# A decode attention kernel: GpSimd instead of SyncE coordinates the entry and the exit of its critical section

## Chip, cores and metric

One core of one Trainium2 chip. The metric is device time in microseconds (us), the median of several executions. The "span" of a profile runs from the first to the last recorded instruction and is some 2 us shorter than the time. The threshold is 2%, which is 13 us here.

## The reference

```python
# x: (2, 1, 512); k_cache, v_cache: (2, 32, 8192, 128) bf16; wq: (512, 4096); wo: (4096, 512)
def reference(A_x, A_k_cache, A_v_cache, A_wq, A_wo, B_x, B_w1, B_w2):
    xn = layernorm(A_x)
    q = (xn @ A_wq) split into 32 heads
    p = softmax(q @ k_cache^T * 128 ** -0.5)
    attention = (p @ v_cache, heads joined) @ A_wo
    mlp = relu(xn @ B_w1) @ B_w2
    return A_x + attention + mlp
```

This is one decode step: the caches, 268 MB, are read once, and little is computed with each byte.

## The kernel before

The whole body stands in one critical section: there the author places instructions and semaphores on the engines by hand, and the framework adds only an entry and an exit. One engine coordinates these two; without an argument it is SyncE. The parts that matter (cuts marked):

```python
    ctx.enter_context(tc.tile_critical(no_gpsimd_drain=True))      # line 63
    # ... tiles, semaphores
    def load_k(t):
        nc.sync.dma_start(ks[t % R][:], K_all[...]).then_inc(dK[t % R], 16)
    nc.sync.dma_start(vs[1][:], A_wq...).then_inc(dV[1], 16)       # SyncE's first transfer, line 168
    # ... SyncE: all loads of K and V, then
        sp.wait_ge(sE, 1)
        sp.dma_start(out..., osb[:]).then_inc(dO, 16)              # the output, line 201
    # GpSimd: setup (memsets, identity matrices), then
        g.wait_ge(sV, 100)
        for t in range(NP):                                        # 32 small copies
            if t >= R:
                g.wait_ge(sS, t - R + 1)
            g.tensor_copy(q2[t % R][:], qb[:, 2 * t:2 * t + 2]).then_inc(sQ1, 1)
        g.wait_ge(dO, 16).then_inc(sG, 1)     # waits for the output's landing, line 238
    # ... TensorE, VectorE, ScalarE: the computation, in loops over 32 blocks
```

As built, the coordinator does this: at the entry a NOP on it (an instruction that here only waits for or sends a signal) tells all engines that they may start. At the exit it first signals that it is through its own part; every engine then drains and signals back; the coordinator waits for these signals and goes on. After that comes the launch's own ending, on line 587 in the profile: a barrier that GpSimd collects and releases (its "collecting wait" is the wait for the other engines' signals), a clearing of semaphores on GpSimd (EVENT_SEMAPHORE_RANGE_CLEAR), and a second barrier.

## Time and profile before

| | before |
|---|---|
| time, median of 3 runs | 661.26 us (661.19 to 661.27) |
| span of the profile | 659.3 us |
| read from memory | 280.5 MB, DMA share 1.00 at 431 GB/s from 34 to 626 us |
| SyncE's first transfer issued | 0.970 us (ScalarE's 2 KB input at 0.922) |
| output issued / landed | 656.759 / 657.950 us |
| GpSimd's wait for it over / the barrier's collecting wait | 657.974 / 658.257 us |
| from the collecting wait to the end of the span | 1.079 us |

The lines of the profile that this rests on are in the prediction below. Times with three decimals are starts of single records in the trace.

### The profile page before, as it was taken

Reading aid. Unit: us, or ns where it says so; the run is one execution under the profiler, and the core shown is the slowest. Engines: PE = TensorE matmul, PEld = TensorE weight load, DVE = VectorE, ACT = ScalarE, POOL = GpSimd, SP = SyncE. Lnnn points to the kernel's source line nnn. Section 1 sums busy time; section 2 is a strip of 40 time slices with the busy share of each in tenths; the row PEclk is TensorE's granted clock in tenths of the full one; section 3 lists DMA queues with packets and bytes.
Section 4 is the critical chain, followed back from the end, with each engine's and each line's share of the span. In section 5 each row is a group of like instructions: output and inputs, shape, how many; then the busy total and the mean of one; then the engine's idle time right before and its main releaser. Section 6 shows DMA issues by size and latency. Waiting matters only on the chain.

```text
span 659.3 us, 26888 instructions
## 1 busy us (share of the span) xinstructions
PE 562.9 (85%) x12747; PEld 538.3 (82%) x12747; DVE 253.4 (38%) x437; ACT 255.9 (39%) x403; POOL 9.0 (1%) x46
## 2 busy tenths in 40 slices
PE   2998899988799787889888788979787998788796
PEld 0488898988799787888888788978787988788795
DVE  1054344433344343334434334434333444334341
ACT  1043444444334433344343434434243444334340
POOL 1000000000000000000000000000000000000000
PEclk9798899989989898999889899979899989889998
DMA  8999999999999999999999999999999999999996
GB/s 363 447 417 437 419 437 429 431 439 423 439 423 435 431 429 439 423 439 423 435 435 427 441 419 439 427 431 437 425 441 419 439 427 431 437 425 441 421 426 266
DMA packets 10670, 280.66 MB, mean 426 GB/s; under 512 B 1250, under 2 KB 1252, under 8 KB 1828
## 3 DMA queue, kind: packets, MB, share of 16 engines
q1 hardware_dynamic: 10656, 280.50, 99.1%
q8 instruction: 9, 0.15, 0.1%
q14 instruction: 1, 0.01, 0.0%
q10 hardware_dynamic: 4, 0.00, 0.0%
HBM read 280.50 MB, written 0.00 MB: 425 GB/s over the span
## 4 chain that ended last, share of the span: by engine, by line
DMA 56%; PE 39%; ACT 2%; issue 1%; SPq 0%; DVE 0%; ACTq 0%
DMA ks<-in_A_k_cache_dram 50%; PE tp L300 21%; PE Sc L307 11%; DMA w_sb<-in_A_wo_dram 4%; PE ot L320 4%; DMA vs<-in_A_wq_dram 2%; ACT kT L427 2%; PE ot L252 1%; PE Sc L285 1%; PE ot L266 1%; ACT L427 1%; SPq L199 0%; PE Sc L355 0%; PE Sc L358 0%; SPq L194 0%
## 5 line engine op out<-in xcount | busy, mean ns | idle before, releaser
L300 PE MATMUL tp<-identb,ks 128*128 128x128 bf16 x4096 | 326.0, 229 | 68.2 <-DMA ks<-in_A_k_cache_dram 67.4
L427 DVE COPY kT<-tp 128x1024 bf16<-128x1024 bf16 x320 | 219.8, 691 | 325.1 <-PE tp L300 324.9
L300 PEld LDWEIGHTS tp<-identb,ks 128*128 128x128 bf16 x4096 | 257.2, 103 | 72.1 <-DMA ks<-in_A_k_cache_dram 70.5
L427 ACT COPY kT<-tp 128x1024 bf16<-128x1024 bf16 x192 | 194.3, 1012 | 233.4 <-PE tp L300 233.4
L307 PE MATMUL Sc<-q,kT 128*128 128x64 bf16 x4096 | 216.6, 196 | 4.6 <-ACT kT L427 4.6
L307 PEld LDWEIGHTS Sc<-q,kT 128*128 128x128 bf16 x4096 | 178.8, 100 | 7.9 <-ACT kT L427 7.8
L320 PE MATMUL ot<-prm,vs 128*128 128x64 bf16 x4224 | 156.1, 192 | 4.7 <-issue 4.7
L320 PEld LDWEIGHTS ot<-prm,vs 128*128 128x128 bf16 x4224 | 139.0, 97 | 7.5 <-issue 4.9
L542 ACT COPY nm<-Sc 128x2 f32<-128x2 f32 x32 | 5.1, 160 | 118.4 <-PE Sc L358 118.4
L546 ACT ACTIVATE prm<-Sc,nm 64x128 bf16<-64x128 f32 x64 | 25.6, 401 | 4.3
L483 DVE TENSOR_REDUCE mcol<-Sc 64x1 bf16<-64x128 f32 x64 | 18.6, 291 | 17.6 <-PE Sc L307 17.2
L427 ACT ACT_TABLE_LOAD x16 | 20.5, 1283 | 2.2
L252 PE MATMUL ot<-vs,xz 128*16 128x512 bf16 x32 | 9.3, 462 | 8.8 <-DMA vs<-in_A_wq_dram 8.8
L534 ACT COPY OTf<-ot 128x2 f32 x32 | 5.1, 160 | 27.3 <-PE ot L320 27.3
L488 DVE TENSOR_REDUCE mx<-Sc 1x2 bf16<-1x128 bf16 x32 | 8.9, 279 | 16.9 <-PE Sc L355 16.9
L252 PEld LDWEIGHTS ot<-vs,xz 128*16 128x16 bf16 x32 | 3.3, 103 | 14.4 <-issue 12.0
L237 POOL COPY q<-qb 128x2 bf16<-128x2 bf16 x32 | 5.9, 187 | 590.8 <-PE Sc L307 567.5
L546 ACT ACTIVATION_READ_ACCUMULATOR prm<-Sc,nm x64 | 11.8, 185 | 0.0
L457 DVE TENSOR_SCALAR qs<-ot 16x512 bf16<-16x512 f32 x1 | 0.7, 678 | 17.9 <-PE ot L252 17.9
L355 PE MATMUL Sc<-identb,mcol 128*1 128x128 bf16 x32 | 7.0, 217 | 0.0
L285 PE MATMUL Sc<-w_sb,hT 128*2 128x512 bf16 (+1 forms) x16 | 6.0, 544 | 0.1
L358 PE MATMUL Sc<-mx,onesb 1*128 1x2 bf16 x32 | 5.5, 172 | 0.0
(56 smaller groups left out, 38.6 us busy)
## 6 DMA issues: line engine op xcount, KB each, us to landing
ks<-in_A_k_cache_dram SPq DMA_DIRECT2D x32, 4096.0 KB, 26.7
vs<-in_A_v_cache_dram SPq DMA_DIRECT2D x31, 4096.0 KB, 31.3
vs<-in_A_wq_dram SPq DMA_DIRECT2D x1, 4096.0 KB, 12.3
vs<-in_A_v_cache_dram SPq DMA_DIRECT2D x2, 2048.0 KB, 20.0
w_sb<-in_B_w_dram SPq DMA_DIRECT2D x1, 1792.0 KB, 16.1
w_sb<-in_A_wo_dram SPq DMA_DIRECT2D x1, 1792.0 KB, 26.0
w_sb<-in_B_w_dram SPq DMA_DIRECT2D x1, 1536.0 KB, 19.3
w_sb<-in_A_wo_dram SPq DMA_DIRECT2D x1, 896.0 KB, 27.7
```

Of the source, the lines that this page charges most:

```text
L237: g.tensor_copy(q2[t % R][:], qb[:, 2 * t:2 * t + 2]).then_inc(sQ1, 1)
L252: i = pe.matmul(qp, lhsT=xz[:, kt, Z - g * Bsz:Z - g * Bsz + QG * Bsz], rhs=vs[1][:, (kt * QG + g) * 512:(kt * QG + g + 1) * 512], start=( ...
L266: i = pe.matmul(hp[0:HP if j >= FA else P, j, :], lhsT=w1_b[:, kt, j - FA, :] if j >= FA else w1_a[:, kt, j, :], rhs=xz[:, kt, Z:Z + Bsz], ...
L285: i = pe.matmul(y, lhsT=hT[half, j, :], rhs=w2_sb[half, j, :], start=(j == 0), stop=(j == FJ - 1),)
L300: t = pe.transpose(tp[e % 4][:, i, :], ks[r][:, kk * Dh:(kk + 1) * Dh], identb[:])
L307: t = pe.matmul(Sc[r][:, 2 * kk:2 * kk + 2 * REP], lhsT=kT[e % 4][:, i, :], rhs=rep(q2[r][:]), start=True, stop=True,)
L320: t = pe.matmul(ot[r][:, 0:2 * REP], lhsT=vs[r][:, kk * Dh:(kk + 1) * Dh], rhs=rep(prm[r][:, kk, :]), start=(kk == 0), stop=(kk == KB - 1),)
L355: pe.transpose(tr_of(r), mcol[r][:], identb[:]).then_inc(sT, 1)
L427: fn(kT[e % 4][:], tp[e % 4][:]).then_inc(kR[e], 1)
L483: m = v.tensor_reduce(out=mcol[i][half, :], in_=S_of(i)[half, :, u], axis=AX.X, op=ALU.max)
L488: v.tensor_reduce(out=mx[i][:], in_=tr_of(i).rearrange("o (u m) -> o u m", u=2), axis=AX.X, op=ALU.max, negate=True,).then_inc(sX, 1)
L546: x = a.activation(out=prm[i][half, :, u], in_=S_of(i)[half, :, u], func=ACTF.Exp, bias=nm[i][half, u:u + 1], scale=1.0, accum_out=RS[half ...
```

## The change

GpSimd coordinates instead of SyncE. The likely intent: GpSimd has little to do and in any case waits for the output at the end, while SyncE issues nearly all the transfers.

```diff
-    ctx.enter_context(tc.tile_critical(no_gpsimd_drain=True))
+    ctx.enter_context(tc.tile_critical(sync_engine=mybir.EngineType.Pool, no_gpsimd_drain=True))
```

The built programs differ in this: SyncE loses its entry NOP and gets other waits at the end. GpSimd gets the entry NOP and the exit's signal, waits and NOP. The other engines keep their instructions and wait for another semaphore.

## The prediction

> **What bounds the kernel now.** I read four things in this order: the slices of the whole span on the page, a table of four stretches, the chain of waits at both ends, and the records of the few source lines that the change can touch. First the slices, each digit a fortieth of the span:
>
> ```profile
> POOL 1000000000000000000000000000000000000000
> DMA  8999999999999999999999999999999999999996
> ```
>
> The DMA engines are 90% or more busy in 38 of 40 slices; GpSimd (POOL) does its setup in the first slice and then next to nothing. The table of stretches (start:end, length, busy time and number of instructions of each engine, granted clock, DMA share, GB/s) sharpens that:
>
> ```profile
> 0.00:34.00 34.00, 20.70 (x139) 10.23 (x140) 4.16 (x14) 3.34 (x5) 3.44 (x16) 0.90 0.96 402
> 34.00:322.00 288.00, 253.82 (x5891) 247.31 (x5889) 118.81 (x200) 121.15 (x190) 2.80 (x15) 0.95 1.00 431
> 322.00:626.00 304.00, 260.92 (x6064) 254.68 (x6061) 120.81 (x204) 124.07 (x197) 2.80 (x15) 0.94 1.00 431
> 626.00:660.00 34.00, 27.42 (x661) 26.07 (x661) 9.60 (x20) 7.30 (x12) 0.00 (x0) 0.85 0.81 340
> ```
>
> From 34 to 626 us the DMA share is 1.00 at 431 GB/s. The kernel reads 280.50 MB, and 280.50 MB / 431 GB/s = 650.8 us of the 659.3 us span. TensorE is behind, with 88% busy in the second stretch and 86% in the third. So the stream of K and V blocks sets the time. Anything that moves the start of the first transfer moves the whole stream, and anything after the last transfer is added at the end. Everything between is bound by something that the change does not touch.
>
> The chain of waits at the start (start us, length, what) shows what stands ahead of the first transfer:
>
> ```profile
> 0.73 0.02 SPq L63
> 0.75 0.07 issue
> 0.81 0.03 SPq L587
> 0.85 0.12 issue
> 0.97 12.30 DMA vs<-in_A_wq_dram
> ```
>
> Line 63 is the line that the change edits: the critical section. SyncE's NOP of line 63 at 0.73 us signals the entry, SyncE's own branch (line 587) starts at 0.81 and the first weights' transfer is issued at 0.97. At the other end, the last work and the records of lines 63, 238 and 587 (engine operation xcount: duration min/median/max in ns, first and last start in us):
>
> ```profile
> 656.76 0.32 SPq L201 DMA_DIRECT2D out_dram<-osb  x1
> ```
>
> ```profile
> L238 POOLq EVENT_SEMAPHORE  x1: 17/17/17, 658.0 to 658.0; - x1
> ```
>
> ```profile
> L63 SPq EVENT_SEMAPHORE  x3: 17/28/28, 657.1 to 657.5; - x3
> L63 SPq NOP  x2: 18/18/18, 0.7 to 658.1; - x2
> L63 ACTq DRAIN  x1: 8/8/8, 657.2 to 657.2; - x1
> L63 SPq DRAIN  x1: 127/127/127, 657.2 to 657.2; - x1
> L63 POOLq NOP  x1: 13/13/13, 658.1 to 658.1; - x1
> ```
>
> The output is issued at 656.76 us; GpSimd's wait for its landing (line 238) is over at 658.0. The exit work of the other engines (line 63 drains, at 657.2) is done meanwhile, hidden under the output's flight.
>
> **What the Trainium skill says.** "Advanced Engine Details and Errata", section Clock Domains, gives SyncE's and GpSimd's sequencers the same 1.2 GHz, so a NOP or a semaphore instruction should cost the same on either; the trace agrees (an EVENT_SEMAPHORE is 17 ns on both; a NOP 18 ns on SyncE, 13 on GpSimd). "Perfetto Trace Analysis", section Sequencer-only Instruction, says that the profile shows only the execution of such an instruction, and that the wait and the propagation of its semaphore lie outside: the trace agrees (the NOP ends at 0.747 us, other engines' branches start at 0.770), so hops must be counted from start to start, not by durations. "DMA: Bandwidth & Descriptors", section Anatomy of one DMA, puts most of a transfer's fixed cost into the receipt of the write, some 2 us for its own path; here the output of 2 KB, on a SyncE queue, takes 1.19 us from issue to its last landing (656.759 to 657.950). That is the time that hides the old exit.
>
> **The change part by part.** Compared as built, the programs of TensorE, VectorE and ScalarE keep all their instructions and only wait on another semaphore. SyncE loses the entry's NOP and gains waits at its end; GpSimd gains the entry's NOP and the collecting waits of the exit. No instruction of the main loop changes, no transfer is added or moved to another queue. The times below are starts of single records in the trace.
>
> Entry, before: GpSimd already collects the launch barrier and releases it at 0.621; SyncE wakes at 0.664, runs the NOP at 0.729, the others' branches start at 0.770 (41 ns later), SyncE's own at 0.814 (85 ns later, since it waits for its own signal), its DMA at 0.970 (156 ns after the branch). Entry, after: GpSimd runs the NOP itself, with no wake of SyncE between. On GpSimd, a semaphore instruction, two branches and then a NOP are 95 ns apart at the end of this trace (657.974 to 658.069), and a semaphore instruction to the next instruction 78 to 81 ns. With 90 ns as an estimate, the NOP is at 0.621 + 0.090 = 0.711. SyncE now waits for another engine's signal, 40 ns (GpSimd's NOP at 658.069, SyncE's NOP at 658.109): branch at 0.751, DMA at 0.907. That is 0.970 - 0.907 = 0.06 us earlier. GpSimd instead waits for its own signal: branch near 0.711 + 0.085 = 0.796 in place of 0.772, so its setup is 0.02 us later; it is done by 4.3 us and TensorE's next wait, for the weights, ends at 13.3, so this is off the path.
>
> Exit, before: after the landing, GpSimd's wait 657.974, its NOP 658.069, SyncE's NOP 658.109, SyncE's drains 658.162 and 658.225, GpSimd's collecting wait of the closing barrier 658.257. From NOP to collecting wait 0.19 us. Exit, after: where the NOP stood at 658.069, GpSimd first signals that it has left the section, and only now do the other engines run the drains that were hidden before. Their drains would start 38 to 45 ns later (as after SyncE's signal at 657.144: 657.182 to 657.189) and be seen after another 30 or so, in parallel. GpSimd itself runs in order: signal at 658.069, own NOP 78 ns later (658.147), two waits on two semaphores each. SyncE's such waits stand 74 ns apart (657.419, 657.493); the first 50 ns after the NOP (658.197), the second at 658.273, the last NOP at 658.35, a branch and a drain at 658.40, the collecting wait 79 ns after (as 659.074 to 659.153), about 658.48. Against 658.257 this is 0.22 us later. SyncE's own new waits (two, 74 ns each, and two drains) end near 658.41 by the same steps, so GpSimd sets it. The 0.9 us from there to the end (barrier, clearing of semaphores, barrier) is the same.
>
> Sum: -0.06 + 0.22 = +0.16 us. 661.26 + 0.16 = 661.42, say 661.4 us, a change of 0.02%.
>
> **The rivals.** (a) The saving at the entry counts and the exit costs nothing, because the other engines' drains are as good as free and GpSimd is quicker through its waits than I took from SyncE: -0.06 us, 661.2. For it: GpSimd was already the last to arrive, waiting for the output; against it: the round trip through the other engines is now serial, after the landing. (b) GpSimd is slow as a coordinator, with some 0.2 us for each step instead of 0.08, as its 157 ns drain in the closing barrier hints: six steps at 0.12 more would add 0.7 us, 662.1. Against it: its semaphore instructions stand 78 to 81 ns apart, the same as SyncE's 74. (c) The 0.06 us shift at the start moves the phase between TensorE and the transfers, or the granted clock falls otherwise (mean 0.938), and the stream loses or wins some tenths. Against it: the DMA share is 1.00 for 592 us, so the phase has little to give, and three runs lie within 0.08 us of each other. It could give 0.5 us either way. (d) The old exit held the span by SyncE's 127 ns drain, which would vanish: against it, that drain ended at 657.35, over 0.6 us before GpSimd's wait.
>
> **Range and chances.** The known parts span 661.2 (a) to 662.1 (b); rival (c) adds a few tenths on either side and favours neither. I take 660.7 to 662.2 for 8 in 10. 2% would be 13 us; both ends together, from the start of the span to the first transfer and from the output's issue to the end, are 0.97 + 2.58 = 3.55 us, so a gain of 2% can not come out of them at all, and a loss would need a hang-like delay. Faster 0.01, same 0.98, slower 0.01.
>
> **What would show it.** In the profile after: the first SyncE DMA near 0.91 us instead of 0.97; the NOP of line 63 at the entry on GpSimd near 0.71; the line 63 drains of ScalarE, VectorE and TensorE no longer at 657.2, under the output's flight, but just after GpSimd's line 238 wait; from that wait's start to the end of the span 1.36 us (657.974 to 659.336) grown to about 1.58; DMA share still 1.00 at 431 GB/s in the two middle stretches, and the output's issue 0.06 us earlier. The prediction is wrong if the exit grows by less than 0.1 or over 0.5 us, if SyncE's first DMA is not earlier, or if the output's issue moves by over 0.3 us, which would mean that the stream itself changed.

## The result

The changed kernel takes 661.96 us (median of 5 runs, 661.83 to 662.06), before 661.27 us in the same rounds (5 runs, 661.19 to 661.34). The ratio, the mean time of one kernel's fast runs over that of the other's of the same rounds and so not quite the ratio of these medians, is 1.0009, 95% interval 0.9997 to 1.0022: the same within 2%. The medians differ by 0.69 us where 0.16 was expected.

The table of stretches after the change (columns as in the prediction) shows the same stream:

```profile
34.00:322.00 288.00, 251.75 (x5903) 245.15 (x5900) 119.07 (x201) 121.54 (x190) 2.80 (x15) 0.96 1.00 431
322.00:626.00 304.00, 260.83 (x6067) 254.54 (x6063) 120.90 (x204) 124.07 (x197) 2.80 (x15) 0.94 1.00 431
```

The chain of waits at the start, of the kernel after:

```profile
0.62 0.02 POOLq L576
0.64 0.06 issue
0.70 0.02 POOLq L63
0.73 0.02 issue
0.74 0.03 SPq L587
0.78 0.12 issue
0.90 12.49 DMA vs<-in_A_wq_dram
```

GpSimd's NOP stands at 0.70 us and follows directly on its release of the launch barrier (line 576, at 0.62); SyncE's first transfer is issued at 0.90 in place of 0.97. At the other end, the output and the records of lines 238 and 63 after:

```profile
656.66 0.32 SPq L201 DMA_DIRECT2D out_dram<-osb  x1
```

```profile
L238 POOLq EVENT_SEMAPHORE  x1: 17/17/17, 657.9 to 657.9; - x1
```

```profile
L63 POOLq NOP  x3: 13/13/13, 0.7 to 658.3; - x3
L63 POOLq EVENT_SEMAPHORE  x3: 17/43/43, 658.0 to 658.2; - x3
L63 SPq DRAIN  x1: 7/7/7, 658.0 to 658.0; - x1
L63 ACTq DRAIN  x1: 8/8/8, 658.0 to 658.0; - x1
```

The output goes out 0.10 us earlier than before, and GpSimd's wait for it is over 0.10 us earlier. But ScalarE's drain now stands at 658.0, behind that wait; before, it stood at 657.2, under the output's flight. Up to here all is as reckoned. What was not reckoned is in GpSimd's records of line 587, the launch's ending. First of the kernel before, then after:

```profile
L587 POOLq EVENT_SEMAPHORE  x4: 17/17/17, 658.3 to 659.2; - x4
L587 POOLq DRAIN  x3: 34/41/157, 658.1 to 659.1; - x3
L587 POOLq EVENT_SEMAPHORE_RANGE_CLEAR  x1: 438/438/438, 658.6 to 658.6; - x1
```

```profile
L587 POOLq EVENT_SEMAPHORE  x4: 17/17/17, 658.5 to 659.9; - x4
L587 POOLq DRAIN  x3: 41/157/168, 658.4 to 659.6; - x3
L587 POOLq EVENT_SEMAPHORE_RANGE_CLEAR  x1: 438/438/438, 658.8 to 658.8; - x1
```

Before, the clearing starts at 658.6 and the last of three drains at 659.1; after, at 658.8 and 659.6. The clearing takes 438 ns in both, so a gap has opened behind it: in the records 34 ns before, 396 ns after. The last drain itself takes 168 ns in place of 34 (the minimum of the three, 34, is gone from the line). The waits of SyncE's queue show the same from the other side. Columns: who waited for whom, us in total, times, longest. Before, then after:

```profile
SPq L587 <- PEq L587: 1.0, 2, 0.8
```

```profile
SPq L587 <- PEq L587: 1.6, 2, 1.3
```

SyncE's longest wait in the ending grew from 0.8 to 1.3 us. (The releaser named is the last signal that the profile saw; the wait is for GpSimd's release.)

The span's growth, 660.046 - 659.336 = 0.71 us, comes from the records as follows:

| part | before | after | difference |
|---|---|---|---|
| start of span to SyncE's first transfer | 0.970 | 0.900 | -0.070 |
| that transfer to output's issue | 655.789 | 655.761 | -0.03 |
| output's issue to end of GpSimd's wait for it | 1.215 | 1.218 | 0.00 |
| that wait to the collecting wait of the barrier | 0.283 | 0.583 | +0.300 |
| collecting wait to the end of the span | 1.079 | 1.584 | +0.505 |

The last line is the open question: neither these instructions nor their order differ between the two programs.

### The profile page after: what moved, and what is told of

It is laid out like the page before. It is cut to its first block, busy times and chain, and to the rows that moved or that the text cites. A ratio compares the mean times of both kernels' runs of the same rounds, so it can differ in the third digit from the quotient of the medians.

```text
span 660.0 us, 26890 instructions
## 1 busy us (share of the span) xinstructions
PE 560.9 (85%) x12747; PEld 535.7 (81%) x12747; DVE 253.2 (38%) x437; ACT 255.9 (39%) x403; POOL 9.0 (1%) x46
## 4 chain that ended last, share of the span: by engine, by line
DMA 55%; PE 40%; ACT 2%; issue 1%; SPq 0%; DVE 0%; ACTq 0%; POOLq 0%
DMA ks<-in_A_k_cache_dram 49%; PE tp L300 21%; PE Sc L307 11%; PE ot L320 4%; DMA w_sb<-in_A_wo_dram 4%; DMA vs<-in_A_wq_dram 2%; ACT kT L427 2%; PE ot L252 1%; PE Sc L285 1%; PE ot L266 1%; ACT L427 1%; SPq L199 0%; PE Sc L355 0%; SPq L194 0%; PE Sc L358 0%
```

## The experiments

Two theories for the half microsecond. **Theory I** (instruction supply): GpSimd's program became five instructions longer and passes a point at which the engine must wait for more instructions. **Theory R** (role): it comes of GpSimd's being the coordinator, its extra waits and signals just ahead of the clearing. Line 587 of before.py stands on other lines in the experiments, as their edits move it. In each experiment the kernel before ran on the same chip in the same rounds.

**e1: before, with five memsets more.** SyncE coordinates; GpSimd only has a longer program.

```diff
+    pad = sb([P, 5], f32, "pad")
 ...
+        for i in range(5):
+            g.memset(pad[:, i:i + 1], 0.0)
         g.wait_ge(sV, 100)
```

> The kernel before (SyncE coordinates), with five 128x1 memsets more on GpSimd after its setup, in a stretch where GpSimd is idle; its program is then 74 instructions long, as in the changed kernel (69 before). Theory I (instruction supply): the 0.4 us gap between GpSimd's semaphore clearing and its last drain in the changed kernel is GpSimd running out of fetched instructions because its program is 5 longer. Then the gap appears here too, without any change of coordinator: gap 0.40 us in place of 0.03, span from GpSimd's collecting wait to the end 1.58 us in place of 1.08, time 661.27 + 0.50 = 661.8 us. Theory R (role): the gap comes from GpSimd's being the coordinator (its waits and notifications at the exit). Then the gap stays 0.03 us and the time 661.3 us.

Measured: 661.74 us (661.44 to 662.00) against 661.23. GpSimd's drains of the ending, in its profile:

```profile
L590 POOLq DRAIN  x3: 41/157/167, 658.4 to 659.7; - x3
```

The 34 ns drain is gone here too; the gap behind the clearing is 393 ns, and from the collecting wait to the end 1.581 us against 1.584 in the changed kernel. The exit proper, from the wait to the collecting wait, stayed at 0.284. Theory R falls: the delay comes without any change of coordinator.

**e2: after, with five memsets fewer on GpSimd** (moved to VectorE).

```diff
-        g.memset(onesh[:], 0.0).then_inc(sG, 1)
 ...
-        g.memset(prm[0][:], 0.0).then_inc(sG, 1)
-        for u in range(2):
-            g.memset(onesh[u * HP:(u + 1) * HP, u, :], 1.0).then_inc(sI, 1)
-        g.memset(ident2[:], 0.0).then_inc(sG, 1)
+        g.wait_ge(sD, 5)              # the same five memsets on VectorE, at its start
-        pe.wait_ge(sI, 5)
+        pe.wait_ge(sI, 3)
```

> The changed kernel with five setup memsets moved from GpSimd to VectorE, so that GpSimd's program has 69 instructions again, as before; coordinator still GpSimd. Theory I: the gap before the last drain goes back to 0.03 us, from the collecting wait to the end 1.08 us, and the time is 661.96 - 0.50 = 661.46 us (what the prediction had reckoned, 661.42). Theory R: gap stays 0.40 us, time 662.0 us.

Measured: 661.39 us (661.37 to 661.55) against 661.23.

```profile
L586 POOLq DRAIN  x3: 34/41/157, 658.2 to 659.1; - x3
```

The gap is 34 ns again and collecting wait to end 1.081 us; the exit proper is still 0.582. With e1 this shows that the 0.50 us follow the length of GpSimd's program and the 0.30 us the coordinator.

**e3: after, with twenty memsets more on GpSimd**, the edit of e1 with 20 in place of 5.

> The changed kernel with twenty 128x1 memsets more on GpSimd after its setup, where it is idle (94 instructions). Theory I: the point in the program where the supply runs out is at a fixed count, so it moves twenty instructions back from the end, into the loop of copies in which GpSimd waits for 20 us at a time, and costs nothing there: gap 0.03 us, time 661.46 us. A variant of theory I in which simply a longer program costs more: gap 0.4 us or more, time 662.0 or above. Theory R: gap stays 0.40 us, time 662.0 us.

Measured: 661.22 us (661.13 to 661.52) against 661.23.

```profile
L590 POOLq DRAIN  x3: 34/41/157, 658.2 to 659.1; - x3
```

The gap is gone (35 ns), though the program is twenty longer than the changed kernel's, and the time is that of before. So length as such does not cost; that the delay is still there, hidden in the loop of copies, is how I read it, and is not shown by this run.

**e4: after, with SyncE waiting for the output's landing** in place of GpSimd.

```diff
         sp.dma_start(out..., osb[:]).then_inc(dO, 16)
+        sp.wait_ge(dO, 16).then_inc(sE, 1)
 ...
-        g.wait_ge(dO, 16).then_inc(sG, 1)
```

> The changed kernel with the wait for the output's landing moved from GpSimd to SyncE, which issued it: GpSimd leaves the section early, so the drains of TensorE, VectorE and ScalarE are hidden under the output's flight again; GpSimd's program is 73 instructions long. By the step times of the changed kernel: from the start of the wait's record to the collecting wait 0.37 us, against 0.58 in the changed kernel and 0.28 before. If the serial round trip is what the exit cost beyond the gap, the time is 661.96 - 0.21 = 661.75 us with the gap (theory I: 73 is still over the limit, or 661.25 if it is not), and about 661.3 under theory R if GpSimd's late start of the exit is what brings the gap.

Measured: 661.42 us (661.19 to 661.75) against 661.23. From the wait to the collecting wait 0.390 us (0.37 expected): the drains of the other engines are hidden again, and that part of the cost goes. GpSimd's program is one instruction shorter here, and the delay came exactly one instruction later. The last drain follows the clearing after 34 ns, and now the collecting wait behind that drain starts 440 ns after it, where 79 is usual.

**e5 and e6: the limit to the instruction.** e5 moves only the three onesh memsets of e2's edit to VectorE (71 instructions on GpSimd); e6 adds one memset to e5 (72).

> The changed kernel with three setup memsets moved from GpSimd to VectorE: GpSimd's program has 71 instructions. So far the delay came between the 71st and the 72nd instruction of GpSimd's program, counted from its start (in the changed kernel and with five more memsets before the last drain, with SyncE's wait one instruction later in the closing code). Theory I with the limit at 71: the program just fits, no delay in the span: 0.03 us before the last drain, 79 ns from that drain to the collecting wait, 78 ns from there to the release; 1.08 us from collecting wait to the end. If the limit is lower or the delay belongs to the closing code, a gap of 0.4 us shows somewhere in it.

> The same with one 128x1 memset more on GpSimd: 72 instructions. Theory I with the limit at 71: the delay comes between the last two instructions of the program, the second collecting wait and the release: about 0.44 us between their starts in place of 0.08, so 1.44 us from the first collecting wait to the end. Any theory in which the delay belongs to an operation (the clearing of semaphores, the drain) expects it where it was, before the last drain, or not at all.

Measured, e6: the last two records of GpSimd, the second collecting wait and the release, start 444 ns apart in place of 78, as expected. Its records in the ending, of which the last drain starts at 659.3 and the release at 659.8:

```profile
L591 POOLq EVENT_SEMAPHORE  x4: 17/17/17, 658.4 to 659.8; - x4
L591 POOLq DRAIN  x3: 34/41/158, 658.1 to 659.3; - x3
```

e5: no delay of GpSimd in the span; 34, 79 and 78 ns as expected. So in programs of 72 to 74 instructions GpSimd's delay comes between the 71st and the 72nd. One expectation missed: in both kernels the first collecting wait came 0.81 us after GpSimd's wait in place of 0.58. VectorE was late for it: its drain of the ending took 134 ns and started at 658.5, where the changed kernel has all of VectorE's drains at 10 ns, the first at 658.1. The line of e5:

```profile
L588 DVEq DRAIN  x2: 10/72/134, 658.5 to 658.9; - x2
```

The edit had lengthened its program from 69 to 72 instructions. It too seems to have such a point near its end; e2, which gives VectorE five more, shows no delay of it. e5 also took 662.04 us with a span of only 659.7. That difference, 2.29 us by the exact span, was more than any kernel's so far, and it pointed at something behind the span:

| kernels | GpSimd's instructions | time less span, mean (lowest to highest) |
|---|---|---|
| before, 27 runs with e1 to e12 | 69 | 2.03 (1.96 to 2.15) |
| e2 | 69 | 2.04 (1.97 to 2.15) |
| e5 | 71 | 2.3 (one run) |
| after; e1; e4; e6 | 74; 74; 73; 72 | 1.83; 1.78; 1.80; 1.83 |
| e3 | 94 | 1.83 (1.78 to 1.89) |

**e7: before, with twenty memsets more on GpSimd; e8: after, with twenty more and with ScalarE waiting for the output.** e7 is the control of e3; e8 is a trial to keep the entry's gain without the other costs.

```diff
 # e8; e7 has only the memsets
+            g.memset(pad[:, i:i + 1], 0.0)       # for i in range(20)
-        g.wait_ge(dO, 16).then_inc(sG, 1)
 ...
+        a.wait_ge(dO, 16).then_inc(sA, 1)        # end of ScalarE's program
```

> The kernel before with twenty memsets more on GpSimd, 89 instructions; a control for the changed kernel with twenty more. Theory I: no delay at the end, as the point of refill lies in the loop of copies: 1.08 us from collecting wait to end, an instruction fetch of 8192 bytes in the loop, five instructions later than the one at 123.3 us in the changed kernel with twenty more, so some 90 us later (five copies of about 18 us). Time 661.25 us, as before.

> The changed kernel with the wait for the output's landing on ScalarE in place of GpSimd, and twenty memsets more on GpSimd (93 instructions): a trial of a version that keeps the entry's gain and loses neither the supply delay nor the late drains. By the step times of the run with SyncE's wait: wait to ScalarE's drain 72 ns, 31 to GpSimd's second collecting wait, 87 to its NOP, 47 to its drain, 80 to the collecting wait of the barrier: 0.32 us, against 0.28 before, 0.39 with SyncE's wait and 0.58 in the changed kernel; no supply delay. With the entry's 0.07 us this is 661.27 - 0.07 + 0.04 = 661.24 us, not to be told from the kernel before.

Measured: e7 661.04 us (660.94 to 661.15), e8 661.01 us (660.90 to 661.39), before 661.26 (661.07 to 661.68). Neither shows a delay in the ending. e8's exit is 0.308 us from wait to collecting wait (0.32 expected). Both are about 0.2 us faster than I expected, and the time less span says why: 1.79 and 1.80 us against 2.02 for the kernel before of the same rounds, with no overlap (1.74 to 1.89 against 1.96 to 2.07). So the kernel before pays some 0.23 us behind the end of its span that twenty memsets more on GpSimd take away. I read this as part of the same delay; why 69 instructions pay half of what 71 do (e9) stays open. Another expectation missed: e7's additional instruction fetch lies at 138.3 us, 15 us after e3's at 123.3, not some 90 us. I had miscounted: of the five instructions that e7 lacks against e3 only the entry's NOP stands ahead of the copies. In the traces the fetch does follow the count: it starts 3.5 to 4.5 us after GpSimd's 52nd recorded instruction in e3, e7, e8 and e12, which is the seventh copy with the NOP (e3, e8) and the eighth without it (e7, e12). It is the 52nd, though, and not the 72nd; what sets this count I do not know.

**e9: before, with two memsets more** (71 instructions, VectorE unchanged).

> The kernel before with two memsets more on GpSimd: 71 instructions, no more work moved to another engine. The run with 71 instructions had no delay within the span but took 2.29 us more than its span, where kernels of 69 take about 2.03 more and kernels of 72 and over about 1.80. If the delay simply falls to the next instruction that GpSimd runs, behind the end of the span, and is fully paid there, then this kernel's span stays at 659.2 to 659.3 us and its time is 0.25 us over that of before: 661.5 us, time less span about 2.3 us. If only time inside the span counts, 661.25 us.

Measured: 661.56 us (661.37 to 661.76) against 661.24, with a mean span of 659.24 against 659.28. The time less span is 2.29 us (2.26 to 2.36). Against the 1.80 of kernels whose delay is not behind the span, this is 2.29 - 1.80 = 0.49 us, as much as the 0.50 seen inside: at 71 instructions the delay seems to fall just outside the span and to be paid fully.

**e10 and e11: the changed kernel and e1 once more,** on another load, without an edit.

> The changed kernel once more, on another load. The terms found so far make -0.07 (entry) + 0.30 (exit) + 0.50 (delay in the span) - 0.24 (delay no longer behind the span) = +0.49 us, 661.75 us; the first measurement said 661.96. If the 0.2 us left over are variation of the stream from load to load, this run lies nearer 661.75; if they belong to the change, it is 661.9 to 662.0 again.

> The kernel before with five memsets more once more, for the same question: the terms are +0.50 - 0.24 = +0.26 us, 661.5 us; the first measurement said 661.74. Variation of the stream: nearer 661.5; a cost of its own of a 74-instruction program: 661.7 again.

Measured: e10 661.78 us (661.68 to 662.01), e11 661.55 us (661.34 to 661.61), before 661.24. The records of the ending are the same to some nanoseconds (gap 401 and 398 ns, collecting wait to end 1.589 and 1.586 us). Both times fell by 0.2 us from the first measurement and now agree with the sum of the terms, 661.75 and 661.5. So the 0.2 us left over in the first measurements are not shown to belong to the change; the mean span of e1's program was 659.94 us in one set of runs and 659.70 in the other.

**e12: before, with twenty memsets more on GpSimd and twenty on VectorE.**

```diff
+        for i in range(20):
+            v.memset(padv[:, i:i + 1], 0.0)
         v.wait_ge(sF, 3)
```

> The kernel before with twenty memsets more on GpSimd and twenty on VectorE, in its idle time before the loop. The run with three memsets moved to VectorE showed a delay of VectorE too. If VectorE also pays behind the span in the kernel before, moving its point away gives a little more than the 0.22 us that GpSimd's gave: time less span under 1.79 us, time 660.9 us or below. If VectorE's delay is hidden there, 661.0 us as with GpSimd's alone; if VectorE's point falls inside its loop and costs, over 661.1.

Measured: 661.11 us (660.86 to 661.29) against 661.24; time less span 1.85 us, near the 1.79 to 1.83 of the other kernels with twenty more on GpSimd. Moving VectorE's point as well brought no gain; 661.11 us lies on the border of the last two cases that I had named, so it does not tell them apart.

## Why the prediction was right, and where its working was not

By its range (660.7 to 662.2) the prediction held at 661.96, and its "the same within 2%" held. By its own working it was right for part of the reasons only: its sum, 661.42, has nothing of the 0.50 us found in the ending, and the result stayed in the range because that had been made wide for rivals (b) and (c). That is luck. Its own test, that it is wrong "if the exit grows by less than 0.1 or over 0.5 us", was failed: from GpSimd's wait to the end of the span it grew from 1.362 to 2.167 us, by 0.81.

- **The stream sets the time and is untouched.** Right: DMA share 1.00 at 431 GB/s in both middle stretches.
- **Entry, -0.06 us.** Right: -0.070. In all profiles with GpSimd as coordinator the first transfer is issued at 0.889 to 0.900 us, with SyncE at 0.956 to 0.970.
- **Exit, +0.22 us: the drains come out from under the output's flight and the round trip becomes serial.** The mechanism was right (e4 and e8 take the cost away in large part by moving the wait). The size was off: +0.30 in place of +0.22. I had taken SyncE's steps: 50 ns from the NOP to the first wait on two semaphores, 74 to 77 from each such wait to the next record. On GpSimd these steps are 92, 92 and 86 ns, the waits' records last 43 ns in place of 28, and from the exit's signal to its own NOP it is 96 ns against 78. From the signal to the collecting wait this makes 0.499 us where I had 0.41.
- **"The 0.9 us from there to the end (barrier, clearing of semaphores, barrier) is the same."** This is the step that failed. The instructions are the same, but their place in GpSimd's program is not: the five instructions more push the ending over a count of 71, and the step from the 71st to the 72nd instruction costs 0.36 us of waiting and, where it falls ahead of the drain, 0.14 in the drain and the step behind it: 0.50 us. I compared the programs instruction by instruction, wrote down which were added, and never counted them. The 0.9 us was also misread: from the collecting wait to the end it is 1.079 us before the change; this slip did not enter the sum.
- **The rest of the sum.** The kernel before already pays some 0.2 us behind its span, so the change does not add all of it to the time. The terms: -0.07 + 0.30 + 0.50 - (2.03 - 1.83) = +0.53 us. The second measurement gave 661.78 - 661.24 = +0.54, the first +0.69. What made the difference between the two is not shown; it came with another load.
- **Rivals.** (b), GpSimd as a slow coordinator, came near in size (662.1), but not by its cause: e1 has the 0.50 us with SyncE as coordinator, and GpSimd's slower steps as coordinator made only 0.08 us more than reckoned, not 0.7. The prediction's remark that a NOP costs the same on both engines does not fit its own figures (18 ns on SyncE, 13 on GpSimd). (a) and (d) fell with the +0.30. (c) was right about a few tenths of variation that belong to no cause that I could name.

What is shown and what is not: that the delay in the ending depends on the number of GpSimd's instructions ahead of it and not on the coordinator is shown (e1, e2, e4, e6; e3 takes it away). That it is a wait for instructions to be fetched is not shown, only the likeliest reading. The page's list of DMA queues (packets, MB, share) has an instruction fetch more in the span of the changed kernel; before, then after:

```profile
q14 instruction: 1, 0.01, 0.0%
```

```profile
q14 instruction: 2, 0.02, 0.0%
```

It is not an additional fetch. The record of transfers goes on behind the span, and has two fetches at the end in both kernels: at 659.672 and 660.912 us before, both behind the span's end at 659.336, and at 659.928 and 660.322 after, the first within the span. With twenty memsets more on GpSimd one of the two is gone from there (e7: 659.785 alone), with twenty on VectorE too both are (e12). So a fetch goes with each engine's count, but in the changed kernel none of them is the one waited for: 659.928 is 0.29 us after the gap is over. In the kernels with twenty more the fetch in the loop does not lie where the 72nd instruction is run either. What GpSimd does in these 0.36 us stays open. One rival was not tested: every timed run here was profiled too (each has a span), so a delay of the recording itself, if that also goes by the number of instructions, is not excluded.

## What to carry to other kernels

Handing the bookkeeping of a section to another engine moves instructions, and here the steps behind the output's landing were serial: ask which steps were hidden under the last transfer and whether the new coordinator is the one that waits for it. Count the instructions of each engine as well as comparing them, since the program that passed the 71st in its last steps paid for it here, while twenty idle instructions more in an idle stretch took the cost away (e7 with 661.04 and e8 with 661.01 us are the fastest kernels here, some 0.2 us or 0.03% below the kernel before, far less than the verdict can separate). And look at time less span beside the span: part of what a change puts into the profile may have been paid outside it before.

## What the Trainium skill lacked or had wrong

- "Runtime: NRT & Kernel Launch", section Instruction fetch mechanics, says of crossing to the next block of instructions that it is "mostly hidden", and speaks of blocks of 16 KiB. If the delay here is such a crossing, it was not hidden at the program's end here: 0.50 us between GpSimd's 71st and 72nd instruction in e1, 0.37 in e6, 0.49 behind the span in e9. Where it fell decided: 69 instructions on GpSimd paid some 0.23 us behind the span, 71 paid 0.49 there, 72 to 74 paid in the span, 89 to 94 showed no such cost. The fetches on one instruction queue of these traces are 16384 bytes, on the other, of which e3 and e7 have one in the loop, 8192.
- "Advanced Engine Details and Errata", section Clock Domains, gives GpSimd's and SyncE's sequencers one clock; the runs agree for simple semaphore instructions (17 ns on both), but a NOP takes 13 ns on GpSimd and 18 on SyncE, and a wait on two semaphores 43 and 28 ns, which no page has.
- No page says what the coordinator of such a section costs at entry and exit: 0.07 us saved at the entry, 0.30 us added at the exit here.
